# One head's store in a linear-attention kernel, cut into sixteen transfers of unequal numbers of rows

## The chip, the core and the metric

The kernel runs on one core of a Trainium2 chip. The core has five engines with instruction streams of their own: PE (TensorE, matmuls), DVE (VectorE), ACT (ScalarE), POOL (GpSimd) and SP (SyncE, which here only issues DMA transfers and waits). Sixteen DMA engines move data between HBM and the on-chip memory. The metric is the device time in microseconds of one execution, the median of several runs.

## The reference

For each of 32 heads of 2048 rows and 128 columns, in bf16:

```python
phi_q = jnp.where(q > 0, q + 1, jnp.exp(q)) + 1e-6
phi_k = jnp.where(k > 0, k + 1, jnp.exp(k)) + 1e-6
kv = jnp.einsum("bhsd,bhse->bhde", phi_k, v)
z = jnp.einsum("bhsd->bhd", phi_k)
num = jnp.einsum("bhqd,bhde->bhqe", phi_q, kv)
den = jnp.einsum("bhqd,bhd->bhq", phi_q, z)[..., None] + 1e-6
return num / den
```

Inputs q, k and v are 512 KB a head each, and so is the output: 67 MB in all cross between HBM and the core.

## The kernel before

A head's 2048 rows lie as 128 partitions of 16 rows: partition p holds rows 16p to 16p+15, 4 KB that are contiguous in HBM. The work on head h is cut into named steps, and each step's name is its operation and the head: `ldk`, `ldq`, `ldv` load the inputs; `ek`, `em` and `rkp` make phi(k) as a sum of two parts (min(exp(k),1)+1e-6 and max(k,0)) on ACT, DVE and POOL; `v1` copies v beside a column of ones; `kv` is the matmuls that accumulate the 128 x 129 matrix of kv and z; `T` transposes q on PE, `eq`, `emq`, `rqa` and `rqb` make phi(q); `n` multiplies it with kv and z; `a` and `r` make the reciprocal of the denominator; `f` multiplies and writes the head's result into one of NO = 12 output buffers (`o_sb`, L445); `st` stores that buffer to HBM (L453).

The order on each engine is written out by hand in the table `ORDER` (L96 to L156). `Program` (L169) turns dependences into semaphore waits: each step adds to its engine's semaphore, and each DMA transfer adds 16 to a semaphore of its buffer (`o0` to `o11` for the stores), as each of the sixteen DMA engines counts one. A wait that another wait already implies is left out.

All loads but one and all stores are issued by SP, in the order of its list. One issue gives one transfer. SP's list ends `... st20.0 ldv31.0 st21.0 st22.0 st23.0 st24.0 st25.0 st26.0 st27.0 st28.0 st29.0 st30.0 st31.0 st31.1 st31.2`: after the last load, of v for head 31, only stores are left. A store is issued when SP has reached it and its head's `f` steps are done. Head h writes to buffer h mod 12, so head 26 uses buffer 2, which no later head writes again. Loads are described to the DMA engines as 32 pieces of 16 KB (L344), stores as 128 rows of 4 KB; head 31 is stored in three parts of 6, 6 and 4 of each partition's 16 rows.

At the end SP waits for every store buffer's semaphore (L469 and L470), two semaphores in an instruction, the last head's buffer last.

Of the kernel before, what the change touches and what calls it, by code (L numbers as in the profile page):

```python
# [6 lines left out]
P = 128  # L7
# [4 lines left out]
NI, NO, NE, NR, NV, NQ, NK = 7, 12, 2, 2, 2, 2, 2  # L12
WARM = (1, 1, 1, 1, 1, 1, 1, 1, 1, 1, 1, 1, 1, 1, 1, 1, 12)
HALVES = ((0, 8), (8, 16))
WHOLE = ((0, 16),)
# [42 lines left out]
def groups(h):  # L58
    if h == NH - 1:
        return ((0, 2, 3, 0), (6, 2, 3, 2), (12, 2, 2, 4))  # L60
    return ((0, 4, 3, 0), (12, 2, 2, 4))


def st_parts(h):
    return ((0, 6), (6, 12), (12, 16)) if h == NH - 1 else WHOLE


# [20 lines left out]
def rqb_parts(h):  # L88
    if na(h) == 16:
        return ()  # L90
    if h == NH - 1:
# [59 lines left out]
        ldk21.0 ldv20.0 ldk22.0 st9.0 ldq20.0 ldv21.0 ldq21.0 st10.0 ldv22.0 ldk23.0 ldq22.0 ldk24.0 st11.0  # L151
        ldv23.0 ldk25.0 ldq23.0 st12.0 ldv24.0 ldq24.0 ldv25.0 st13.0 ldk26.0 ldq25.0 ldv26.0 st14.0 ldk27.0
        ldq26.0 ldv27.0 st15.0 ldk28.0 ldv28.0 ldq27.0 st16.0 ldk29.0 ldq28.0 ldv29.0 st17.0 ldq29.0 ldk30.0
        ldv30.0 st18.0 ldq30.0 ldk31.0 st19.0 ldq31.0 st20.0 ldv31.0 st21.0 st22.0 st23.0 st24.0 st25.0 st26.0
        st27.0 st28.0 st29.0 st30.0 st31.0 st31.1 st31.2
    """,  # L156
}
# [11 lines left out]
class Program:  # L169
# [10 lines left out]
    def add(self, eng, key, fn, deps=(), dma=None, inc=True):  # L180
        assert key not in self.op, key
        self.op[key] = (eng, fn, tuple(deps), dma, inc)
# [71 lines left out]
def bass_standalone__linear_attn_elu__prompt_kernel(nc: bass.Bass, q: bass.AP, k: bass.AP, v: bass.AP, out: bass.AP):  # L254
# [8 lines left out]
    qf, kf, vf, of = (t.rearrange("b h s d -> (b h) s d") for t in (q, k, v, out))  # L263
    rows = lambda t, h: t[h].rearrange("(p j) d -> p j d", j=NT)

    with ExitStack() as es:
# [17 lines left out]
        o_sb = sb([P, NO, NT, D])  # L284
# [7 lines left out]
        pr = Program(sem)  # L292
        add = pr.add
# [58 lines left out]
        def head(h):  # L352
# [58 lines left out]
            for i, (t0, nb, m, b0) in enumerate(groups(h)):  # L411
# [31 lines left out]
                def g(e, t0=t0, t1=t1, nb=nb, m=m, b0=b0):  # L443
# [5 lines left out]
                        in1=_ap(rden_sb[:, :, :], first(rden_sb[:, h % 2, t0:t0 + 1]) - first(rden_sb[:, :, :]),  # L449
                                [[m, nb], [1, m], [0, D]]), op=ALU.mult)  # L450
                add("DVE", f"f{h}.{i}", g, [f"r{h}.{i}"] + freed(NO, h, ("st", st_parts)))
            for i, (a, b) in enumerate(st_parts(h)):
                add("SP", f"st{h}.{i}", lambda e, a=a, b=b: e.dma_start(rows(of, h)[:, a:b], o_sb[:, h % NO, a:b]),  # L453
                    [f"f{h}.{j}" for j, (t0, nb, m, b0) in enumerate(groups(h)) if t0 < b and a < t0 + nb * m],
                    dma=f"o{h % NO}")

        for h in range(NH):
            head(h)
# [7 lines left out]
        for e, engine in (("POOL", nc.gpsimd), ("SP", nc.sync), ("ACT", nc.scalar), ("PE", nc.tensor), ("DVE", nc.vector)):  # L466
            pr.emit(e, engine)
        last = f"o{(NH - 1) % NO}"
        for name in [f"o{s}" for s in range(NO) if f"o{s}" in pr.count and f"o{s}" != last] + [last]:  # L469
            nc.sync.wait_ge(pr.get(name), pr.count[name])  # L470


# [26 lines left out]
```

## Time and profile before

| what | value |
|---|---|
| median of 3 runs | 169.22 us (169.18 to 169.33) |
| the profiled execution's own time | 169.27 us |
| its span, from the first to the last instruction | 168.0 us |
| mean granted clock of TensorE | 0.991 |
| read from and written to HBM | 50.33 and 16.78 MB |
| store of a whole head, median from issue to landing | 19.9 us |
| parts of the last head's store, from issue to landing | 2.7 and 3.2 us |

The page of the profile shows one execution. Its first table gives each engine's busy time, its share of the span and the number of instructions; PEld is the weight load, which overlaps the matmuls. The second cuts the span into 40 equal slices, with the busy share of each in tenths (9 is 90% or more). The third lists the DMA queues. The fourth is the chain of work that ended last, followed back from the last instruction to what released it. SPq and PEq are an engine's sequencer, which issues and waits without counting as busy. "Landing" is the moment at which the last of a transfer's sixteen semaphore steps arrives; the trace also holds the time of each single step and of each DMA packet, but not the number of the DMA engine that it belongs to. Names of steps (st26, f31.2) are put to instructions by their place in the order.

### The profile page before, as it was taken

The page shows a single profiled execution, that of the slowest core. Times are in us where ns is not written, and L with a number is a line of the kernel's source. Part 1 is how long each engine was busy: PE and PEld are TensorE (multiplying, and loading weights), DVE is VectorE, ACT ScalarE, POOL GpSimd, SP SyncE. Part 2 cuts the span into 40 slices and gives each one's busy share as a digit, 9 for nine tenths or more (in the row PEclk, how much of TensorE's full clock was granted, in tenths as well). Part 3 has the DMA queues.
Part 4 walks back from the last instruction along what each step waited for, and adds up shares of the span by engine and source line. Part 5 has one row for each costly group of instructions (what it writes and reads, how often), then busy time and mean ns, then how long its engine had stood idle before and what let it go on. Part 6 is the DMA issues. An engine that isn't in the chain of part 4 may idle for free.

```text
span 168.0 us, 6186 instructions
## 1 busy us (share of the span) xinstructions
PE 156.5 (93%) x2716; PEld 150.8 (90%) x2716; DVE 151.9 (90%) x300; ACT 149.7 (89%) x102; POOL 93.2 (55%) x71
## 2 busy tenths in 40 slices
PE   6967999999999999999999999999999989999940
PEld 2456999999999999999999999999999989999840
DVE  0339799999999999999999999999999989999992
ACT  3499899999999999999999999999999979995800
POOL 1397676555555666665555556666655356642000
PEclk9999999999999999999999999999999999999996
DMA  5999999999999999999999999999999999999985
GB/s 207 433 418 414 394 425 386 421 416 410 414 410 425 402 410 396 429 405 431 395 425 419 409 414 430 407 415 419 421 419 423 404 421 436 397 421 409 401 329 216
DMA packets 9819, 67.51 MB, mean 402 GB/s; under 512 B 2080, under 2 KB 2464, under 8 KB 6816
## 3 DMA queue, kind: packets, MB, share of 16 engines
q1 hardware_dynamic: 9648, 66.59, 96.8%
q8 instruction: 21, 0.34, 0.8%
q10 hardware_dynamic: 144, 0.52, 0.8%
q14 instruction: 6, 0.05, 0.1%
HBM read 50.33 MB, written 16.78 MB: 400 GB/s over the span
## 4 chain that ended last, share of the span: by engine, by line
DVE 74%; PE 15%; DMA 4%; issue 3%; ACT 1%; SPq 0%
DVE la L445 36%; DVE la L400 10%; DVE la L364 10%; DVE la L407 9%; PE la L382 7%; DVE la L441 4%; DMA la<-in_k_dram 4%; DVE la L387 3%; PE la L423 3%; PE la L394 3%; PE la L425 3%; DVE la L438 2%; ACT la L361 1%; ACT la L398 1%; SPq L349 0%
## 5 line engine op out<-in xcount | busy, mean ns | idle before, releaser
L371 POOL TENSOR_SCALAR la<-la 128x2048 bf16<-128x2048 bf16 (+1 forms) x32 | 59.9, 1873 | 55.2 <-PE la L382 44.9
L445 DVE TENSOR_TENSOR la<-la 128x1536 bf16<-128x1536 f32 (+2 forms) x65 | 77.7, 1196 | 0.1
L423 PE MATMUL la<-la 128*128 128x129 bf16 x512 | 67.0, 219 | 0.2 <-DVE la L387 0.2
L425 PE MATMUL la<-la 128*128 128x129 bf16 x512 | 67.0, 219 | 0.0
L382 PE MATMUL la<-la 128*128 128x129 bf16 x1024 | 63.3, 220 | 2.0 <-POOL la L375 1.4
L361 ACT ACTIVATE la<-la 128x2048 bf16<-128x2048 bf16 (+1 forms) x33 | 61.3, 1859 | 4.3 <-DMA la<-in_k_dram 4.3
L398 ACT ACTIVATE la<-la 128x2048 bf16<-128x2048 bf16 (+2 forms) x35 | 60.2, 1730 | 4.4 <-PE la L425 2.7
L382 PEld LDWEIGHTS la<-la 128*128 128x128 bf16 x1024 | 59.3, 98 | 2.5 <-issue 1.7
L425 PEld LDWEIGHTS la<-la 128*128 128x128 bf16 x512 | 49.5, 97 | 0.0
L423 PEld LDWEIGHTS la<-la 128*128 128x128 bf16 x512 | 47.9, 97 | 0.4 <-DVE la L387 0.4
L375 POOL COPY la<-la 128x1024 int32<-128x1024 int32 (+1 forms) x33 | 34.1, 1037 | 5.9 <-DMA la<-in_v_dram 5.9
L394 PE MATMUL la<-la 128*128 128x128 bf16 x512 | 34.0, 219 | 1.3 <-DVE la L387 0.9
L404 ACT ACTIVATE la<-la 128x1024 bf16<-128x1024 bf16 (+1 forms) x32 | 33.5, 1046 | 0.0
L394 PEld LDWEIGHTS la<-la 128*128 128x128 bf16 x512 | 29.9, 98 | 2.7 <-DVE la L387 1.0
L400 DVE TENSOR_SCALAR la<-la 128x2048 bf16<-128x2048 bf16 (+2 forms) x35 | 24.0, 687 | 4.5 <-ACT la L398 4.5
L364 DVE TENSOR_SCALAR la<-la 128x2048 bf16<-128x2048 bf16 (+1 forms) x33 | 23.7, 718 | 1.1 <-ACT la L361 1.1
L418 PE MATMUL la<-la 128*128 128x3 bf16 (+1 forms) x128 | 21.6, 168 | 1.3 <-DVE la L445 1.3
L407 DVE TENSOR_SCALAR la<-la 128x1024 bf16<-128x1024 bf16 x31 | 20.5, 661 | 0.0
L441 DVE RECIPROCAL la<-la 128x12 f32<-128x12 f32 (+2 forms) x65 | 13.0, 201 | 1.6 <-PE la L425 0.6
L418 PEld LDWEIGHTS la<-la 128*128 128x128 bf16 x128 | 12.5, 98 | 1.5 <-DVE la L445 1.5
L330 PE MATMUL la<-la 128*128 128x480 bf16 x28 | 7.8, 428 | 1.5 <-POOL la L315 1.5
L387 DVE CAST la<-la 128x129 bf16<-128x129 f32 x32 | 7.7, 240 | 0.8 <-PE la L382 0.8
(16 smaller groups left out, 11.4 us busy)
## 6 DMA issues: line engine op xcount, KB each, us to landing
la<-in_k_dram SPq DMA_DIRECT2D x32, 512.0 KB, 19.6
la<-in_q_dram SPq DMA_DIRECT2D x32, 512.0 KB, 19.7
la<-in_v_dram SPq DMA_DIRECT2D x31, 512.0 KB, 19.6
out_dram<-la SPq DMA_DIRECT2D x31, 512.0 KB, 19.9
la<-in_v_dram ACTq DMA_DIRECT2D x1, 512.0 KB, 5.3
out_dram<-la SPq DMA_DIRECT2D x2, 192.0 KB, 2.7
out_dram<-la SPq DMA_DIRECT2D x1, 128.0 KB, 3.2
```

The source lines that it names most:

```text
L361: add("ACT", f"ek{h}.{i}", lambda e, a=a, b=b: e.activation(em_sb[:, h % NE, a:b], k_sb[:, h % NI, a:b], ACT.Exp), over("ldk", h, ld_parts ...
L364: add("DVE", f"em{h}.{i}", lambda e, a=a, b=b: e.tensor_scalar(em_sb[:, h % NE, a:b], em_sb[:, h % NE, a:b], 1.0, EPS, op0=ALU.min, op1=AL ...
L371: add("POOL", f"rkp{h}.{i}", lambda e, a=a, b=b: e.tensor_scalar(rk_sb[:, h % NR, a:b], k_sb[:, h % NI, a:b], BIG, 0.0, op0=ALU.min, op1=A ...
L375: add("POOL", f"v1{h}.{i}", lambda e, a=a, b=b: e.tensor_copy(v1_sb[:, h % NV, a:b, 0:D].bitcast(i32), v_sb[:, h % NI, a:b].bitcast(i32)), ...
L382: ins = e.matmul(kv_ps, lhsT=src[:, j], rhs=v1_sb[:, h % NV, j, 0:NC], start=(j + part == 0), stop=(j == NT - 1 and part == 1))
L394: ins = e.transpose(xT[:, j], q_sb[:, h % NI, j], ident[:])
L398: add("ACT", f"eq{h}.{i}", lambda e, a=a, b=b: e.activation(emq_sb[:, h % NQ, a:b], xT[:, a:b], ACT.Exp), over("T", h, t_parts, a, b) + fr ...
L400: add("DVE", f"emq{h}.{i}", lambda e, a=a, b=b: e.tensor_scalar(emq_sb[:, h % NQ, a:b], emq_sb[:, h % NQ, a:b], 1.0, EPS, op0=ALU.min, op1 ...
L407: add("DVE", f"rqb{h}.{i}", lambda e, a=a, b=b: e.tensor_scalar(rq_sb[:, h % NQ, a:b], xT[:, a:b], 0.0, None, op0=ALU.max), over("eq", h, ...
L423: e.matmul(to, lhsT=emq_sb[:, h % NQ, t], rhs=kvs_sb[:, h % NK, 0:NC], start=late and c == 0, stop=False, skip_group_check=True)
L425: ins = e.matmul(to, lhsT=rq_sb[:, h % NQ, t], rhs=kvs_sb[:, h % NK, 0:NC], start=False, stop=True, skip_group_check=True)
L445: return e.tensor_tensor(out=_ap(o_sb[:, :, :, :], first(o_sb[:, h % NO, t0, 0:1]) - first(o_sb[:, :, :, :]), [[m * D, nb], [D, m], [1, D] ...
```

## The change

The store of head 26 (the 27th) goes in sixteen transfers, one after the other on SP, where it went in one. The first has partition 0 alone, the next 2 partitions, then 3, and so on up to 15 (partitions 0 to 119), and the last one has the 8 that remain. Each has a semaphore of its own (`o2.0` to `o2.15`), for which SP also waits at the end. The first piece waits for the head's `f` steps as the whole store did; the others need no wait, as the first one's implies theirs.

```diff
+ROWS = tuple((i * (i + 1) // 2, (i + 1) * (i + 2) // 2) for i in range(15)) + ((120, P),)
+
+
+def st_rows(h, i):
+    return ROWS[i] if h == 26 else (0, P)
+
+
 def st_parts(h):
+    if h == 26:
+        return WHOLE * len(ROWS)
     return ((0, 6), (6, 12), (12, 16)) if h == NH - 1 else WHOLE
...
-        ldv30.0 st18.0 ldq30.0 ldk31.0 st19.0 ldq31.0 st20.0 ldv31.0 st21.0 st22.0 st23.0 st24.0 st25.0 st26.0
+        ldv30.0 st18.0 ldq30.0 ldk31.0 st19.0 ldq31.0 st20.0 ldv31.0 st21.0 st22.0 st23.0 st24.0 st25.0 st26.0 st26.1 st26.2 st26.3 st26.4 st26.5 st26.6 st26.7 st26.8 st26.9 st26.10 st26.11 st26.12 st26.13 st26.14 st26.15
...
             for i, (a, b) in enumerate(st_parts(h)):
-                add("SP", f"st{h}.{i}", lambda e, a=a, b=b: e.dma_start(rows(of, h)[:, a:b], o_sb[:, h % NO, a:b]),
+                add("SP", f"st{h}.{i}", lambda e, a=a, b=b, p=st_rows(h, i): e.dma_start(
+                    rows(of, h)[p[0]:p[1], a:b], o_sb[p[0]:p[1], h % NO, a:b]),
                     [f"f{h}.{j}" for j, (t0, nb, m, b0) in enumerate(groups(h)) if t0 < b and a < t0 + nb * m],
-                    dma=f"o{h % NO}")
+                    dma=f"o{h % NO}" if h != 26 else f"o{h % NO}.{i}")
...
         last = f"o{(NH - 1) % NO}"
-        for name in [f"o{s}" for s in range(NO) if f"o{s}" in pr.count and f"o{s}" != last] + [last]:
+        for name in [name for name in pr.count if name[0] == "o" and name != last] + [last]:
             nc.sync.wait_ge(pr.get(name), pr.count[name])
```

## The prediction

> **What bounds the kernel now.** I read four views in turn: the table of shares and the forty slices, the chain that ended last, the windows of the last 12 us, and SP's issues with the landings of what they issue.
>
> The slices first. DVE, PE and ACT are at nine tenths, and so are the DMA engines from the second slice to the next-to-last one.
>
> ```profile
> span 168.0 us, 6186 instructions
> PE 156.5 (93%) x2716; PEld 150.8 (90%) x2716; DVE 151.9 (90%) x300; ACT 149.7 (89%) x102; POOL 93.2 (55%) x71
> DMA  5999999999999999999999999999999999999985
> DMA packets 9819, 67.51 MB, mean 402 GB/s; under 512 B 2080, under 2 KB 2464, under 8 KB 6816
> q1 hardware_dynamic: 9648, 66.59, 96.8%
> DVE 74%; PE 15%; DMA 4%; issue 3%; ACT 1%; SPq 0%
> ```
>
> The chain is DVE's, but it ends with DVE's last instruction, f31.2, at 164.71 us; the span ends at 168.0. What lies between is the landing of the last stores. The windows show that the DMA engines work on after the other engines stop (columns: busy time and count of PE, PEld, DVE, ACT, POOL; clock; DMA share; GB/s):
>
> ```profile
> 156.00:160.00 4.00, 3.21 (x56) 2.85 (x53) 3.75 (x11) 3.11 (x4) 0.00 (x0) 1.00 0.98 396
> 160.00:164.00 4.00, 2.09 (x36) 1.91 (x36) 3.86 (x10) 0.00 (x0) 0.00 (x0) 1.00 0.81 329
> 164.00:168.00 4.00, 0.00 (x0) 0.00 (x0) 0.71 (x2) 0.00 (x0) 0.00 (x0) 0.61 0.54 202
> ```
>
> The stores of the tail, as SP issues them (start, us taken), and the median time to landing:
>
> ```profile
> 144.73 1.17 SPq L453 DMA_DIRECT2D out_dram<-la  x1
> 149.52 0.33 SPq L453 DMA_DIRECT2D out_dram<-la  x1
> 158.34 0.33 SPq L453 DMA_DIRECT2D out_dram<-la  x1
> 161.68 0.33 SPq L453 DMA_DIRECT2D out_dram<-la  x1
> 164.74 0.33 SPq L453 DMA_DIRECT2D out_dram<-la  x1
> out_dram<-la SPq DMA_DIRECT2D x31, 512.0 KB, 19.9
> SPq L470 <- DMA out_dram<-la: 2.5, 2, 1.5
> ```
>
> They are st26 (the one that is changed), st27, st29, st30 and st31.2. By the trace's record of landings they land at 161.41, 162.80, 165.37, 166.62 and 167.93. So st26 lies 16.7 us in the queue, and the queue never empties before the end: each whole store lands 1.17 to 1.40 us after the one before it, and st31's three parts (1.31 us in all) follow st30 without a hole. Each transfer's semaphore gets sixteen steps, one from each DMA engine, and these tell that the engines are not level. For st26 they lie 4.97, 4.90, 4.76, 4.57, 4.31, 4.13, 3.07, 1.76, 1.60, 1.16, 0.39, 0.29, 0.28, 0.24, 0.09 and 0 us before the last one. For st30 the six fast engines, which by then wait for work, are 2.3 to 2.45 us early, and the ten others 1.94, 1.83, 1.39, 1.29, 0.59, 0.58, 0.52, 0.50, 0.31 and 0. The slow engines' backlog sets the end: the last step of st31.2 comes 1.34 us after its first, and without a backlog all sixteen would have come with that first one. This is the most that any relief of the queue could gain.
>
> **The change, part by part.** One issue of 128 rows of 4 KB becomes sixteen, of 1 to 15 and 8 rows. The bytes are the same; no other engine's list changes.
>
> *SP's issues.* st26 took 1.17 us, behind thirteen transfers that had not landed; the four stores issued with ten or fewer outstanding took 0.33. With 0.04 between issues, sixteen pieces take 16 x 0.37 = 5.9 us at the lower end and 16 x 1.21 = 19.4 at the upper; a gain is excluded, as fifteen issues are added. Behind them on SP's queue stand only st27 to st31 and the waits of the end; no load is left, and no DVE instruction waits for st26 (buffer 2 isn't used again). st27's data is ready at 149.49. At the lower end it is issued at 150.6, 1.1 us late, which costs nothing: the engine that ends last reaches st27 only at 161.41, and the first packet of st30 started 0.83 us after its issue, so st27 may be issued as late as 160.6. That allows (160.6 - 144.73)/16 = 0.99 us for a piece. I take a value near the lower end, as a piece has 8 rows on average against 128, and what blocks an issue depends on rows rather than on a count: at 37.45 a store behind thirteen transfers, eleven of them loads of 32 packets, took 0.34, whereas st26 behind as many, eight of them stores of 128, took 1.17. The term is 0.
>
> *Which engine gets the rows.* A whole store gives each engine 8 packets of 4 KB and one step of its semaphore: 8 x 0.155 + 0.006 = 1.25 us, by the packets' records. No transfer of fewer than 128 rows is in this trace. One end: the pieces are dealt on evenly, 8 rows for each engine, and nothing changes. The other: each piece gives one row to each engine, beginning with the same one every time. Then that engine has 16 rows and 16 steps, 16 x 0.161 = 2.58 us, 1.33 more than before; its neighbours 15, 14 and so on, so the first eight get 1.33, 1.17, 1.01, 0.85, 0.69, 0.53, 0.36 and 0.20 us more, and the last eight 0.12, 0.28, 0.44, 0.60, 0.76, 0.92, 1.08 and 1.25 less. I take the second, since every one of the 129 transfers on record begins anew with all sixteen engines and nothing shows a memory from one to the next. [...]
>
> *What of that reaches the end.* The trace doesn't number the engines, so I deal the sixteen differences at random onto the sixteen lags of st30. The six fast engines absorb anything: 1.33 is less than their 2.3. Over all deals the latest engine moves by 0.74 us in the middle, 0.27 at one tenth and 1.17 at nine tenths. All of it lies on the path, as st27 to st31 only queue behind it. The term is +0.74.
>
> *A step for each row.* Nearest row: the steps of st31.1 and st31.2 on one engine follow each other by 8 x 0.042 + 0.006 = 0.34 us without a stall; a step itself takes 0.009. Pieces give a step every 0.16 us. Lower end: nothing beyond the 0.006 already counted. Upper end: a step can't come faster than 0.34, so 16 x 0.34 = 5.4 us on the busiest engine, 4.2 more than now. I take the lower: the packet after a step starts 6 ns after it in all the records. [...]
>
> *The waits at the end.* SP waits for 28 semaphores instead of 12, two in an instruction: 14 instead of 6, some 0.07 us apart. Most are behind landings that come earlier; after st30's landing six remain, 0.4 us, under the 1.31 us until st31.2 lands. Without that cover eight more would cost 0.56. The term is 0.
>
> Sum: 0 + 0.74 + 0 + 0 on the profiled execution's 169.27 us (span 168.0 and 1.27 around it) is 170.01. The median of the runs is 0.05 lower, which gives 169.96: 170.0.
>
> **The rivals.** *Hidden (within 0.34 us, 169.2).* The pieces are dealt evenly, or the engines that get more are fast ones. For it: seven of sixteen engines have 3 us to spare at st26. Against it: eight engines get more, and nine are slow.
>
> *Faster (168.7 to 168.9).* All engines that end last are among those that get fewer rows. The latest is relieved by up to 1.25 us; the next ones stand 0.31 and 0.50 behind it, and one that is itself relieved a little gives 0.3 to 0.6. It decides if none of the six latest is among the first eight. For it: nothing but that the engines are unnumbered. Against it: by chance that is about 1 in 280, though lags may be tied to places.
>
> *SP's issues become the bound (170.9 to 172.9).* If each piece takes the 1.04 us that most issues took in the full queue (with 0.04 between), st27 goes out at 162.0, its packets start at 162.8 instead of 161.4, and the four stores, st31 and 0.47 for the last receipt follow: 162.8 + 5.0 + 1.3 + 0.47 = 169.6, +1.7. At st26's 1.17 it is +3.7. It decides from 0.99 us a piece. For it: 1.17 on st26 itself. Against it: the weight by rows above.
>
> *Steps become the bound (up to 173.4).* The 4.2 us above, if the busiest engine is the latest.
>
> **How the numbers follow.** Forecast 0.58, hidden 0.17, faster 0.06, SP's issues 0.12, steps 0.07. A measurement of this kernel tells about 0.2% (0.34 us) from no change: faster 0.06, same 0.17, slower 0.77. The forecast's own range is 169.5 to 170.6. The range for all, 169.1 to 171.4, takes in the hidden case and the lower half of SP's and leaves out 0.19.
>
> **What would show it.** Right: sixteen short issues from 144.7 on, st27 issued near 150 to 151, DVE's last instruction still at 164.7, and the steps of st27 to st31.2 spread wider, the last one 0.3 to 1.3 us later. Wrong: st27 issued after 160 (SP's issues), steps of one engine 0.3 us apart (steps), a spread as before (hidden), or less packets on the last engine (faster). A DVE end that moves would make the whole account wrong.

## The result and the profile after

The changed kernel takes 170.12 us (median of 4 runs, 170.02 to 170.34), beside 169.20 us (169.18 to 169.33, now 4 runs too) for the kernel before on the same chip. The ratio is 1.0054, with a 95% interval of 1.0037 to 1.0072: slower by 0.92 us. The profiled execution took 170.34 us, its span 169.0.

The page of the changed kernel, the lines that answer to those of before:

```profile
span 169.0 us, 6209 instructions
PE 156.6 (93%) x2716; PEld 150.9 (89%) x2716; DVE 152.1 (90%) x300; ACT 149.7 (89%) x102; POOL 93.3 (55%) x71
DMA  5999999999999999999999999999999999999983
DMA packets 9931, 67.51 MB, mean 399 GB/s; under 512 B 2192, under 2 KB 2576, under 8 KB 6928
q1 hardware_dynamic: 9760, 66.59, 96.4%
DVE 74%; PE 15%; DMA 4%; issue 3%; ACT 1%; SPq 0%
```

The engines' busy times are those of before within 0.2 us. The bytes are the same; SP's queue (q1) holds 9760 packets where it held 9648. These 112 are the steps (the packets under 512 B rise by as many, from 2080 to 2192): the sixteen pieces give 1 + 2 + ... + 15 + 8 = 128 of them, the whole store gave 16.

The windows of the end of the changed kernel (busy time and count of PE, PEld, DVE, ACT, POOL; clock; DMA share; GB/s):

```profile
156.00:160.00 4.00, 3.18 (x56) 2.83 (x53) 3.87 (x11) 3.09 (x4) 0.00 (x0) 1.00 0.98 382
160.00:164.00 4.00, 2.09 (x36) 1.92 (x36) 3.86 (x10) 0.00 (x0) 0.00 (x0) 1.00 0.87 340
164.00:169.00 5.00, 0.00 (x0) 0.00 (x0) 0.69 (x2) 0.00 (x0) 0.00 (x0) 0.62 0.44 165
```

PE, DVE and ACT do here what they did before, at the same moments. Only the DMA engines differ: they move 382 GB/s and not 396 from 156 to 160 us, at the same share of 0.98, so a part of the busy time moves fewer bytes; and they work past 168 us.

SP's issues in the changed kernel (start, us taken): the first two pieces, the piece of 15 rows, this one together with the last piece, then st27, st30 and st31.2; the last instruction of DVE; and SP's wait for landings at the end (us, times, longest):

```profile
144.76 0.31 SPq L462 DMA_DIRECT2D out_dram<-la  x1
145.12 0.24 SPq L462 DMA_DIRECT2D out_dram<-la  x1
149.72 0.39 SPq L462 DMA_DIRECT2D out_dram<-la  x1
149.72 0.73 SPq L462 DMA_DIRECT2D out_dram<-la  x2
150.50 0.36 SPq L462 DMA_DIRECT2D out_dram<-la  x1
161.65 0.33 SPq L462 DMA_DIRECT2D out_dram<-la  x1
164.72 0.57 SPq L462 DMA_DIRECT2D out_dram<-la  x1
163.14 1.56 DVE L454 TENSOR_TENSOR la<-la 128x768 bf16<-128x768 f32 x2
SPq L480 <- DMA out_dram<-la: 2.9, 2, 1.9
```

The pieces are issued in 5.7 us, no wait stands in between, and DVE ends at 164.70, as before (164.71). The landings that follow, by the trace's record of steps (us; first and last of the sixteen):

```
            before             after
st25        155.23 to 160.15   155.21 to 160.40
st26        156.44 to 161.41   last piece to 163.07
st27        157.68 to 162.80   156.88 to 163.94
st30        164.17 to 166.62   164.17 to 167.67
st31.2      last 167.93        last 169.00
```

The three parts of st31 share one semaphore, so their steps can't be told apart there, and for st31.2 only the last one is given. The first step of st30 stands where it stood, its last is 1.05 us later, and that of st31.2 1.07. The loss is wholly in how unevenly the engines finish.

**Which rows go where.** The steps of the pieces answer this. A few pieces, each with the time of its issue and all its steps (of the 15 rows some are left out):

```
1 row   144.76   145.19 | 155.45
2 rows  145.12   145.53 | 155.65 156.11
3 rows  145.40   145.83 | 155.84 156.23 156.30
5 rows  146.01   146.49 | 156.21 156.59 156.66 157.58 160.24
7 rows  146.70   147.17 | 156.59 156.94 157.01 157.94 158.77 160.63 161.22
8 rows  147.04   147.52 | 155.42 156.77 157.12 157.19 158.13 158.97 160.84 161.43
15 rows 149.72   150.27 | 156.60 156.93 158.07 158.39 ... 161.51 162.26 162.87
```

Ahead of the bar stands one record half a microsecond after the issue, ten microseconds before any row moves; behind it as many steps as the piece has rows. Each piece brings in one new engine, and the engines of the earlier pieces return at equal distances (155.45, 155.65, 155.84 and so on), so this is a staircase that begins with the same engine each time. What the early record stands for, no run shows.

So the pieces number the engines, which a trace of whole stores can't: e0 is the engine that every piece uses, e1 the one that the second piece adds, and so on, and e15 the one that no piece uses. In that numbering the last steps of st25, which no piece precedes, were (us):

```
e0 155.27  e1 155.93  e2 156.04  e3 157.20  e4 160.06  e5 158.39  e6 160.40  e7 155.21
e8 155.35  e9 159.99  e10 160.03 e11 159.89 e12 158.36 e13 158.52 e14 158.81 e15 155.65
```

The engine that gets most, e0, is 5 us ahead of the latest. What counts is e4 and e6, late already and with 12 and 10 rows in place of 8.

### The profile page after: what moved, and what is told of

Read it like the earlier page. It is cut to its first block, busy times and chain, and to the rows that moved or that the text cites. A ratio compares the mean times of both kernels' runs of the same rounds, so it can differ in the third digit from the quotient of the medians.

```text
span 169.0 us, 6209 instructions
## 1 busy us (share of the span) xinstructions
PE 156.6 (93%) x2716; PEld 150.9 (89%) x2716; DVE 152.1 (90%) x300; ACT 149.7 (89%) x102; POOL 93.3 (55%) x71
## 2 busy tenths in 40 slices
DMA packets 9931, 67.51 MB, mean 399 GB/s; under 512 B 2192, under 2 KB 2576, under 8 KB 6928
## 3 DMA queue, kind: packets, MB, share of 16 engines
q1 hardware_dynamic: 9760, 66.59, 96.4%
## 4 chain that ended last, share of the span: by engine, by line
DVE 74%; PE 15%; DMA 4%; issue 3%; ACT 1%; SPq 0%
DVE la L454 36%; DVE la L409 10%; DVE la L373 10%; DVE la L416 9%; PE la L391 7%; DVE la L450 4%; DMA la<-in_k_dram 4%; DVE la L396 3%; PE la L432 3%; PE la L403 3%; PE la L434 3%; DVE la L447 2%; ACT la L370 1%; ACT la L407 1%; SPq L358 0%
```

## The experiments

The questions were, in this order: is it the placement of rows or the number of transfers; do the semaphores cost anything; does a lag last to the end; and can a cut that relieves the late engines beat both kernels. All edits are made against the changed kernel, SP's list being fitted to the number of pieces; the diffs are shortened. `ROWS` gives the first partition of each piece and the one after its last. The experiments ran on three chips, each beside the kernel before, whose median lay between 169.19 and 169.21 us.

### Same number of packets, other places

```diff
-ROWS = (1, 2, 3 ... 15 and 8 partitions)
+ROWS = eight pieces of 16 partitions        # first kernel
+ROWS = sixteen pieces of 8 partitions       # second kernel
```

> Theory A (placement: a transfer of n rows, n up to 16, gives one row to each of the first n DMA engines, and the end is set by the engines that lag most; by the changed kernel's steps these are engines 4, 6, 9, 10 and 11, with 0, 1, 2, 7, 8 and 15 two us or more ahead). Eight transfers of 16 rows give every engine 8 rows and 8 steps, as the whole store did with one step: 7 x 0.006 = 0.04 us more. Expected 169.2 to 169.4 us. Rival B (each additional transfer costs the queue something, whatever engine it is on: 0.92 us over 15 additional transfers = 0.061 us each): 7 x 0.061 = 0.43, so 169.6 us.

> As many transfers, issues and semaphores as the changed kernel has, all of 8 rows. Theory A: engines 0 to 7 get 16 rows and 16 steps, 1.33 us more, among them the late engines 4 and 6; engines 8 to 15 get none. Expected +1.3 us, 170.4 to 170.7 us, more than the changed kernel. Rival B: 15 additional transfers as in the changed kernel, 170.1 us. Rows dealt on evenly from where the last transfer stopped: 169.2 us.

Eight pieces of 16: 169.39 us, ratio 1.0012 (1.0003 to 1.0020), 0.19 us slower than before. Sixteen pieces of 8: 170.69 us, ratio 1.0081 (1.0068 to 1.0094), 1.49 us slower. The queue's line of the two pages, with the span, first for the pieces of 16:

```profile
span 168.1 us, 6197 instructions
q1 hardware_dynamic: 9760, 66.59, 96.9%
```

And for the pieces of 8:

```profile
span 169.4 us, 6209 instructions
q1 hardware_dynamic: 9760, 66.59, 96.1%
```

Both have the 9760 packets of the changed kernel, byte for byte the same amount, and so 128 steps. With 8 rows on every engine they cost 0.19 us; with 16 rows on e0 to e7 and none on the others 1.49. By the arithmetic of the staircase the difference should be 8 x 0.161 = 1.29 us on e4 and e6: measured 170.69 - 169.39 = 1.30. These two kernels differ in the number of transfers too, but the changed kernel has as many as the one with pieces of 8 and takes 0.57 us less (170.12): the number alone doesn't set the time, the placement does. The packets of st31.2 show it as well, the only ones of 1 KB that SP's queue moves at the end: with the pieces of 8 fourteen engines are through with them by 166.97, the last two at 168.69 and 168.92.

### One semaphore for all pieces

```diff
-dma=f"o{h % NO}" if h != 26 else f"o{h % NO}.{i}")
+dma=f"o{h % NO}")
```

> The changed kernel's sixteen transfers of 1 to 15 and 8 rows, all on the one semaphore of the buffer as before the change, so SP waits for 12 semaphores at the end instead of 28. Theory A: the semaphores cost nothing, 170.0 to 170.3 us. Rival C (the waits and semaphores are what costs): back to 169.2 to 169.5 us.

Measured 170.11 us, ratio 1.0059 (1.0043 to 1.0074), the changed kernel's own time within 0.01 us. Sixteen semaphores and eight more waits at the end cost nothing that can be seen.

### The same staircase on head 10

```diff
-ROWS for head 26
+ROWS for head 10 (the same sixteen pieces)
```

> The sixteen unequal transfers on the store of head 10 instead of head 26, in the middle of the run with loads behind them. Theory A: the queue never empties, so what engines 4 and 6 are given there they still carry at the end: 169.6 to 170.1 us; SP's 5 us of issues are covered by the some 18 us of transfers that are queued. Rival (the engines level out over the later transfers, only the tail counts): 169.2 us. Rival (loads come late behind the issues): DVE's last instruction later than 165.5, 170.3 us and more.

Measured 169.84 us, ratio 1.0037 (1.0024 to 1.0051), 0.63 us slower than before. Span and last DVE instruction of this kernel:

```profile
span 168.7 us, 6216 instructions
163.37 1.55 DVE L454 TENSOR_TENSOR la<-la 128x768 bf16<-128x768 f32 x2
```

The pieces move at about 100 to 104 us. DVE ends at 164.92, 0.2 us later than in the kernel before, which is too little for the result; the six microseconds of extra issues, which here stand ahead of the loads from v of head 22 on, are hidden but for that. The lag stays with the engines: the sixteen steps of st25, some 55 us after the pieces, come at 154.47 to 160.85, where the kernel before has 155.23 to 160.15. The first is 0.76 us earlier and the last 0.70 later, as in a queue that never empties in between (the DMA slices of this kernel's page are at 9 from the second to the 38th).

### All rows on one engine

```diff
+ROWS = ((0, 127), (127, 128))
```

> Head 26's store as 127 rows and 1 row. If a transfer uses the largest number of engines up to 16 that divides its rows, 127 (a prime) go all to engine 0: 127 x 0.155 = 19.7 us there, after 155.3, then 1 row and the stores of heads 27 to 31 on it, 4 x 1.25 + 1.31 + 0.47: the span ends near 182, 183 us in all. The fifteen others are relieved of 8 rows but don't matter. If rows are dealt to all engines whatever their number: 169.2 us.

Measured 184.07 us (one run), 14.9 us slower. The record of the steps shows one engine for each of the two transfers: each has one step soon after its issue and one with its data, the larger one at 145.32 and 176.26. The slices and two windows of this kernel, and SP's issues (the second line has both transfers of head 26, the third st27):

```profile
span 182.8 us, 6188 instructions
DMA  5999999999999999999999999999999999529300
160.00:164.00 4.00, 2.09 (x36) 1.92 (x36) 3.86 (x10) 0.00 (x0) 0.00 (x0) 1.00 0.21 85
172.00:176.00 4.00, 0.00 (x0) 0.00 (x0) 0.00 (x0) 0.00 (x0) 0.00 (x0) 0.50 0.16 50
144.89 0.31 SPq L462 DMA_DIRECT2D out_dram<-la  x1
144.89 17.58 SPq L462 DMA_DIRECT2D out_dram<-la  x2
162.52 0.38 SPq L462 DMA_DIRECT2D out_dram<-la  x1
```

The time was near what was expected (a span of 182.8 us where near 182 was said), for one engine with 127 rows at 0.159 us works 20 us. What was not expected is the second issue: one row, and it took SP 17.2 us. Until 162.47 SP could do nothing else, st27 went out at 162.52 and not at 149.5, and at 160 to 164 us the DMA share is 0.21. So a long issue, the condition of the prediction's rival on SP's issues, exists; it came with one engine whose own queue was long, not with the number of issues. Even here it isn't the bound: the last landings are those of the engine with the 127 rows, which had work without a break, and the others are done before 175 us (from 176 to 180 us the DMA share is 0.07, about one engine of sixteen).

### A cut that relieves the late engines

The staircase shows how up to 15 rows are dealt. For the cut the author assumed that 51 partitions go on three engines (17 rows each), 64 on sixteen (4 each) and 13 on thirteen (1 each), beginning with e0 as the pieces do: 22 rows on e0 to e2, which are over 4 us early, 5 on e3 to e12, and 4 on the rest. The second kernel's queue agrees as to the number of engines: 9664 packets, 16 more than before, and so 3 + 16 + 13 = 32 steps in place of 16. Each late engine has 3 rows less, 3 x 0.161 = 0.48 us.

```diff
+ROWS = ((0, 64), (64, 115), (115, 128))     # three engines take partitions 64 to 114
+ROWS = ((0, 51), (51, 115), (115, 128))     # three engines take partitions 0 to 50
```

> Three transfers, of 64, 51 and 13 rows. Theory A, with the largest number of engines up to 16 that divides the rows: 64 rows give each engine 4; 51 = 3 x 17 give engines 0, 1 and 2 seventeen each; 13 give engines 0 to 12 one each. So engines 0 to 2, which are ahead by more than 4 us at this store and have nothing to do later, carry 22 rows instead of 8, and the late engines 5 instead of 8: 3 x 0.155 = 0.46 us less on the path. Expected 168.7 to 168.9 us, faster than the kernel before. Rival B: two more transfers, 0.12 us more, 169.3 us. Rows dealt evenly: 169.2 us.

> The cut of the run with 64, 51 and 13 rows, but with the 51 rows first (rows 0 to 50) and the 64 after them. Placement gives the same as there: engines 0 to 2 get 22 rows, the late ones 5, 0.46 us less, 168.7 to 168.9 us, if no late engine meets a stall. [...] Rival E (the stalls come with any cut whose parts leave the engines unequal, whichever rows): as there, 169.0 to 169.2 us.

The first gave 169.08 us, ratio 0.9997 (0.9985 to 1.0009), no gain: a miss. Its twelve runs spread over 168.76 to 169.70, six of them up to 168.94 and six from 169.21 on. The second gave **168.76 us**, ratio 0.9975 (0.9965 to 0.9985), 0.45 us faster than the kernel before and 1.36 faster than the changed one. Span, queue and windows of the second:

```profile
span 167.5 us, 6190 instructions
q1 hardware_dynamic: 9664, 66.59, 97.1%
156.00:160.00 4.00, 3.24 (x57) 2.89 (x54) 3.91 (x11) 3.15 (x4) 0.00 (x0) 1.00 0.95 385
160.00:164.00 4.00, 2.09 (x36) 1.92 (x36) 3.86 (x10) 0.00 (x0) 0.00 (x0) 1.00 0.91 364
164.00:168.00 4.00, 0.00 (x0) 0.00 (x0) 0.75 (x2) 0.00 (x0) 0.00 (x0) 0.93 0.47 174
```

Where the kernel before moves 396, 329 and 202 GB/s in these windows, this one moves 385, 364 and 174: more of the work before 164 us, less after. Its last landing is at 167.42, against 167.93 before and 169.00 in the changed kernel.

The two cuts ran on different chips, each beside the kernel before; their intervals just touch. What differs between their profiles is in the packets. A row of 4 KB takes 159 ns in the median, in the kernel before and in the changed one. Rows that took over 240 ns, between 154 and 163 us of the one profiled execution:

```
kernel before 3     changed kernel 11     eight of 16: 4     sixteen of 8: 8
partitions 64 to 114 on three engines 16   partitions 0 to 50 on three engines 2
```

The next three runs, on one chip, take the two cuts apart, since partitions, places in HBM and order all differ between them. Each piece is now given by its partitions (first, and the one after the last) and then in the same way by its place in the head's output, in rows of 4 KB. In the second and third kernel the two differ, so there the rows of head 26 come out in another order than the reference's.

```diff
+ROWS = ((51, 115, 51, 115), (0, 51, 0, 51), (115, 128, 115, 128))   # cut of the faster kernel, 64 issued first
+ROWS = ((0, 64, 51, 115), (64, 115, 0, 51), (115, 128, 115, 128))   # partitions of the slower, places of the faster
+ROWS = ((51, 115, 0, 64), (0, 51, 64, 115), (115, 128, 115, 128))   # partitions of the faster, places of the slower
-    rows(of, h)[p[0]:p[1], a:b], o_sb[p[0]:p[1], h % NO, a:b]),
+    rows(of, h)[p[2]:p[3], a:b], o_sb[p[0]:p[1], h % NO, a:b]),
```

> The cut of the fast kernel (rows 0 to 50, 51 to 114, 115 to 127), with the 64 rows issued before the 51; every row in its place. D1 and D2: 168.7 to 168.9 us, as the fast one. F: 169.0 to 169.2 us.

> Head 26's store as 64, 51 and 13 rows in the order of the first such run (169.08 us), from the same partitions (0 to 63, then 64 to 114), but to other places of the output: the 64 go to rows 51 to 114 and the 51 to rows 0 to 50 of the head, so that this head's output rows are in the wrong places. Theory D1 (long rows come from the places in HBM): as with 51 rows first, 168.7 to 168.9 us, few rows over 240 ns. Theory D2 (from the partitions): as the first such run, 169.0 to 169.2 us, some 15 to 20 rows over 240 ns. Theory F (from the order of the transfers): 169.0 to 169.2 us.

> The counterpart: 64 rows from partitions 51 to 114 to rows 0 to 63 of the head's output, then 51 from partitions 0 to 50 to rows 64 to 114, then 13; again this head's rows are in the wrong places. D1: 169.0 to 169.2 us. D2: 168.7 to 168.9 us. F: 169.0 to 169.2 us.

| kernel | partitions on three engines | time, us | ratio | long rows |
|---|---|---|---|---|
| 64, then 51 | 0 to 50 | 168.76 | 0.9974 (0.9964 to 0.9983) | 3 |
| places exchanged | 64 to 114 | 168.83 | 0.9987 (0.9972 to 1.0001) | 10 |
| partitions exchanged | 0 to 50 | 168.77 | 0.9979 (0.9969 to 0.9989) | 5 |

The order of issue does nothing: the first line is the faster kernel again. The partitions exchanged leave the gain whole, so the places in HBM don't decide. In these five profiles, one of each kernel, the long rows go with the partitions: 16 and 10 where three engines read partitions 64 to 114, 2, 3 and 5 where they read 0 to 50. In time none of the three theories came out whole: F missed all three kernels, D1 the third and D2 the second, where it said 169.0 to 169.2 us. That second kernel has runs from 168.56 to 169.70, and its interval reaches from the faster cut's to no gain; its profiled execution, with 10 long rows, was the fastest of them, so the number of long rows alone doesn't give the time; on an engine that isn't among the last ones a long row should, by estimate, cost nothing. Whether the two cuts differ in time on one chip was not settled, and why these partitions should make long rows stays open.

### Two heads with the good cut

```diff
+ROWS = {25: ((0, 51), (51, 115), (115, 128)), 26: ((0, 51), (51, 115), (115, 128))}
```

> The same cut (51, 64 and 13 rows) on the stores of heads 25 and 26. Theory A: the late engines are relieved by 0.92 us, but engines 0 to 2 carry 28 rows more, 28 x 0.155 + 4 x 0.006 = 4.4 us, which is all that engine 2, the last of the three, has to spare: it would end at 156.0 + 4.4 + 7.6 = 168.0 in the span, as the kernel before does. Expected 169.0 to 169.4 us, set by engines 0 to 2. If their room is larger than I read it: 168.3 us.

Measured 170.15 us (169.36 to 171.44), ratio 1.0070 (1.0045 to 1.0096), 0.94 slower: a miss. Span and windows:

```profile
span 168.7 us, 6193 instructions
156.00:160.00 4.00, 3.22 (x57) 2.87 (x53) 3.84 (x11) 3.13 (x4) 0.00 (x0) 1.00 0.91 348
160.00:164.00 4.00, 2.09 (x36) 1.92 (x36) 3.86 (x10) 0.00 (x0) 0.00 (x0) 1.00 0.94 359
```

348 GB/s from 156 to 160 us, where the single cut had 385. It is not that e0 to e2 got too much: they finish their 51 rows of head 26 at 160.07 to 160.85 and with 5 rows more each, at 0.161 us, all of it by about 161.7, while the last step of head 26 is at 162.36 on another engine. What this kernel has more of is long rows: 34, although the three engines read partitions 0 to 50. From 158 to 162 us the packets of SP's queue take 6.0 us more than their usual durations, summed over the engines, against 0.8 in the kernel with one cut and 0.6 in the kernel before. What sets them off was not found.

## Why the prediction was right, step by step

It said 170.0 us and slower; measured were 170.12 and 1.0054. Its own steps:

**SP's issues: term 0, right.** Sixteen pieces at 0.24 to 0.39 us, st27 issued at 150.50 where 150.6 was forecast. The weight by rows was the right reading of the 1.17 us of st26. The run with 127 rows on one engine adds what the whole store hid: an issue was held for 17.2 us behind 127 rows on one engine while the fifteen others had little to do. That the rows waiting on the fullest engine of a transfer are what counts is the author's estimate from this one run.

**Which engine gets the rows: the second end, right.** One row for each engine, the same first engine each time, 16 rows on the busiest and 7 or less on the last eight. The steps show it directly, and the pieces of 16 and of 8, 1.30 us apart with 9760 packets both, confirm it.

**What of that reaches the end: +0.74, the right size, in part by luck.** The trace of before doesn't number the engines, so the sixteen differences were dealt at random. The pieces number them, and the sum can be made. Late engines gain 12 - 8 = 4 rows on e4 (+0.68 us) and 2 on e6 (+0.36). In the kernel before the latest engine goes from 160.15 at st25 to 167.93 at the end. In the changed one e4, the second latest at the end, goes from 160.06 to 168.50. With e4 as the last engine the end would be 0.57 us later, which is placement, and lies inside the 0.27 to 1.17 that the deal allowed. But e6 ends later still. It starts at 160.40 and has +0.36, and its step of the piece of 7 comes at 161.22 and not at 160.6; a row of 766 ns in place of 159 (160.09 to 160.85 by the packets) fits this, +0.61. Five whole stores of 1.25 us (st26 to st30) and st31's 1.31 follow: 160.40 + 0.36 + 0.61 + 7.56 = 168.93, and the last landing is at 169.00. Without that stall e6 would have ended at about 168.4, before e4. So of the 1.07 us between the two profiled executions 0.57 is placement and the last 0.50 a stall, for which the prediction had no term. That the middle of a random deal came near the whole is luck. How the 0.92 of the medians divides can't be told from one execution; the same cut with one semaphore lost 0.91, with 16 long rows in its profile, so the total repeats; its division is not known.

One reading of the prediction was wrong here, though no term changes with it. The 1.34 us between the first and the last step of st31.2 was counted on the semaphore that st31's three parts share, where the parts' steps mix; so was the 2.7 us of the table of before. By the packets of 1 KB the first engine is through with st31.2 at about 165.96 in the kernel before and the last at 167.46, 1.5 us.

**A step for each row: nothing beyond 0.006, right.** A row and its step run every 0.161 us on an engine, as the records of packets have it, and 112 more steps evenly spread cost 0.19 us (0.05 to 0.34) together with seven more transfers. The steps themselves are recorded every 0.19 to 0.21 us, so that they fall behind the rows within the sixteen pieces, but the next whole store makes this up. These 0.19 us are all that shows of a price for each transfer, in a queue that is full.

**The waits at the end: 0, right.** After st30's landing at 167.67 the remaining ones are done 0.3 us later, and the last landing is at 169.00; with one semaphore the time is the same.

**The rivals.** Hidden fell, as e4 and e6, two of the three latest, are among the eight that get more. Faster fell for the same reason here, but its mechanism is real: with the cut of 51, 64 and 13 rows the late engines get less, and 0.45 us is gained, which lies inside its 0.3 to 0.6. SP's issues and steps did not become the bound.

## What to carry to other kernels

In this queue, which never empties before the end, the sixteen DMA engines didn't wait for each other (their steps of st25 lie 5.2 us apart in the changed kernel), and rows more on late ones were paid at the end of the program, and in part also when they were sent 60 us earlier (0.63 us against 0.92); so leave a store like this one whole, or cut it into parts that load all engines alike (eight parts of 16 rows cost 0.19 us, sixteen of 8 rows 1.49). Where the end is a landing, look at the sixteen steps of the last transfers that have a semaphore of their own: an even end can gain no more than their spread, and transfers of a few rows, which ran on as many engines as they had rows here (1 to 15), tell which engine is which. A cut that gives early engines more is worth its trial (51, 64 and 13 here, 0.45 us), but its gain was lost when it was made twice, so each such cut has to be timed.

## What the runs showed that was not expected

**The rows on one engine held the issuer.** The issue of one row behind 127 on one engine took SP 17.2 us, and the fifteen other engines ran short of work meanwhile (a DMA share of 0.21 from 160 to 164 us).

**Rows stall, and how many differs from cut to cut.** From 2 or 3 rows over 240 ns near the end to 34, with the same bytes; single rows take up to 0.79 us. With one head cut the number went with the partitions that three engines read and not with order or place in HBM, by one profile of each kernel, but the two heads with 34 read the partitions that had few. The cause stays open.

**The engines' lags grow through the run.** In the kernel before, the sixteen steps of the first load lie 0.4 us apart, those of st26 4.97. The spread grows by jumps: one engine is 0.97 us behind at 18 us, a second at 25, a third at 32. At these times (17.96, 25.05 and 32.47 us) packets of 16 KB start on the queue that the page calls instruction, which lists 21:

```profile
q8 instruction: 21, 0.34, 0.8%
```

Each takes about 1.06 us (0.94 to 1.11), as much as a jump. That they are the cause is argued from the times alone; no run moved or removed one. It could explain why the late engines seem to be the same ones from kernel to kernel (with the pieces of 8, which load only e0 to e7, two engines end at 168.69 and 168.92 and the rest by 166.97, as e4 and e6 would), and so why a cut can be fitted to them.
